# A branch hint for the final jump, eight separate PSUM banks for the tail's products, and three accumulations handed to ScalarE and GpSimd

## The chip, the core and the metric

The kernel runs on one core of a Trainium2 chip. The core has TensorE (PE in the profile, its weight loads PEld) for matrix products into PSUM, VectorE (DVE) and ScalarE (ACT), which read PSUM and SBUF, GpSimd (POOL), used here on SBUF alone, and SyncE (SP), which issues nearly all DMAs. Each engine has its own queue of instructions and runs it in order; engines wait for each other through semaphores. A jump is an instruction of every engine's queue. The metric is the device time of one launch in microseconds (us), the median over runs.

## What is computed

The input is one sequence of 2048 rows with 512 columns. Two branches read the same x, and a gate mixes them row by row:

```python
g = _sigmoid((x * gate_w).sum(-1, keepdims=True))
a = _A_ref(x, A_wq, A_wk, A_wv, A_wo)   # attention: 32 heads of 16, one k and one v for all heads
b = _B_ref(x, B_w1, B_w2)               # silu(x @ w1) @ w2, 1792 hidden columns
return g * a + (1 - g) * b
```

Attention is softmax(q k / 4) v for each head and then a product with wo (512x512). All inputs and the output are float32.

## The kernel before

Products are made from pairs of float16 parts: every operand is split into a leading part and a rest, and three matmuls (leading by leading, leading by rest, rest by leading) stand for one.

**Two passes.** `first_pass` splits with fixed powers of two as scales. While it runs it collects extreme values, checks them against limits, and writes one integer, `flag`. `second_pass` is the same computation with scales worked out from the data. All engines load `flag` (L1632) and jump (L1633) over the code of `second_pass` if it is 0. It is 0 with these inputs, so a run consists of the first pass, the jump and the end of the program. The second pass is thousands of instructions long, so the jump's target lies far behind the jump.

**The main loop.** The sequence is cut into four chunks `c` of 512 rows, the heads into four groups `o` of eight, each handled in two rounds: 32 rounds (`rounds`) of 16 steps. In a step TensorE makes scores into a tile S (`scores`, L1381), ScalarE exponentiates them (L1387), and TensorE multiplies the result with v into two banks pv (`sums`, L1485). VectorE makes the rests of the exponentials (`low`, L1406). The feed-forward products and the projections with wo fill TensorE's spare slots (`f_slot`, L1027). PSUM has eight banks of 512 float32 per partition: two S tiles of two banks each, the banks pv0 and pv1, and two banks pm.

**Order.** The queues' order is made by a planner in Python that keeps an estimated clock for each engine (`pe[0]`, `dve[0]`, `act[0]`, `pool[0]`). Work for VectorE is entered by `put(duration, ready, due, function)`; `choice` picks the task with the earliest due time. The planner's clocks decide the order alone; on the chip, semaphores decide the times.

**The end of a round.** `norm_a` normalizes a round: `out_of_psum` transposes pv0 and pv1 into T and U (L1303, L1304), `joined` adds and scales (L1309 to L1311), `quotient` divides (L1325 to L1327), and after the second round of a head group `turned` transposes back and splits the result O in two (L1333 to L1336). In the last round (`late`) VectorE does all of it; before, GpSimd does L1309 to L1311, L1335 and L1336. O feeds `out_proj`.

**Outputs.** For each block of 128 output rows there is a tile `acc` in SBUF, to which six products of the last chunk are added in turn: four feed-forward parts (`ffn_o`, gate `g1`), a projection of the first three head groups, and one of the last group (`out_proj`, gate `gg`). `evict_out` enters the addition as a task of VectorE, `add_out` (L1001), which reads the product from PSUM, multiplies it by the gate and adds it to `acc`; after the last part it issues the output's DMA on SyncE's queue (L1004). `parts[n]` counts what a block has, `n_parts(n)` what it needs.

**The tail.** When all scores are issued, a first loop finishes the sums that are left, a second the feed-forward product that is under way, and a third makes the eight last products, each with full 128x128 matmuls (L1031): the last feed-forward part of four row blocks, six matmuls each, and the projections of the last head group, three each. Before each product all of VectorE's open tasks are entered. The generator `spaces` names the PSUM bank that each product goes to: the first banks of two S tiles, their second banks, then two banks pm, then S again. A tile is one unit for the waits, so a product in the second bank of an S tile waits for the readers of its first bank.

Of the kernel before, what the change touches and what calls it, by code (L numbers as in the profile page):

```python
# [6 lines left out]
F32 = mybir.dt.float32  # L7
# [5 lines left out]
AF = mybir.ActivationFunctionType  # L13
OP = mybir.AluOpType
# [159 lines left out]
def kernel(  # L174
# [21 lines left out]
    nc = tc.nc  # L196
    _, S, D = x.shape
# [19 lines left out]
    g1 = consts.tile([128, NKT], F32)  # L217
# [693 lines left out]
    def attention(ctx, scale_of, t_scale, shifts, split_pieces, chores, q_todo, bounds, early, gates_, later):  # L911

        wp = ctx.enter_context(tc.tile_pool(name="wp", bufs=1, reuse_waits="tile"))
        pS = ctx.enter_context(tc.tile_pool(name="pS", bufs=2, space=PSUM, reuse_waits="tile"))
        pO = ctx.enter_context(tc.tile_pool(name="pO", bufs=1, space=PSUM, reuse_waits="tile"))
# [4 lines left out]
        pe, act, dve, pool, turn = [0.0], [0.0], [0.0], [0.0], [0.0]  # L920
# [11 lines left out]
        def put(dur, ready, due, f, hard=False, low=None, turns=False):  # L932

            tasks.append([due, ready, dur, f, hard, low, turns])
            return tasks[-1]

        def pool_until(t):

            while pooled and max(pool[0], pooled[0][0]) <= t:
                ready, dur, f = pooled.pop(0)  # L940
                pool[0] = turn[0] = max(pool[0], ready, turn[0]) + dur
                pool[0] += 0.08
                if f:
                    f(pool[0])

        def on_pool(durs, f=None):
            for n, dur in enumerate(durs):
                pooled.append((dve[0] + 0.1, dur, f if n == len(durs) - 1 else None))

        def do(t):  # L950
            tasks.remove(t)
            dve[0] = max(dve[0], t[1])
            pool_until(dve[0])
            if t[6]:
                dve[0] = turn[0] = max(dve[0], turn[0]) + t[2]
            else:
                dve[0] += t[2]
            t[3]()
# [30 lines left out]
        accs, parts, given = {}, {}, {}  # L989
        n_parts = lambda n: len(GF) + 1 + (n // 4 == NCH - 1)  # L990

        def add_out(c, t, po, gate):
            n = c * 4 + t
            if n not in accs:
                assert n < ACCS or parts[n - ACCS] == n_parts(n - ACCS)
                accs[n] = wp.tile([128, D], F32, name="acc", bufs=ACCS)
            a = accs[n]
            if n not in parts:
                nc.vector.tensor_scalar(a, po, gate[:, n:n + 1], None, op0=OP.mult)
            else:  # L1000
                nc.vector.scalar_tensor_tensor(a, po, gate[:, n:n + 1], a, op0=OP.mult, op1=OP.add)  # L1001
            parts[n] = parts.get(n, 0) + 1
            if parts[n] == n_parts(n):
                nc.sync.dma_start(out[n * 128:n * 128 + 128], a)  # L1004

        def evict_out(c, t, gate):

            def evict(po):
                return put(0.75, pe[0] + 0.2, pe[0] + 0.9, lambda: add_out(c, t, po, gate), True)

            return evict
# [53 lines left out]
        def out_proj(c, O, t):  # L1065
            need(wo, 0)
            given[c] = given.get(c, 0) + 1
            return Out([(lambda i, b, m, n=32, o=o: O[o][b, i, t * 128 + m:t * 128 + m + n],
                         lambda j, b, o=o: wo_s[b, j, o]) for o in O],
                       evict_out(c, t, gg))  # L1070
# [215 lines left out]
        def norm_a(i, pv, rb, key):  # L1286

            while (t := next((v for v in tasks if v[3] is of_v[0]), None)):
                do(t)
            T, U = wp.tile([128, 512], F32, name="T"), wp.tile([128, 512], F32, name="U")  # L1290
            z = U.rearrange("p (a b) -> p a b", b=32)
            if rb == 0:
                state["C"] = wp.tile([128, 16, 32], F32, name="C")
            C = state["C"][:, :, 16 * rb:16 * rb + 16]

            late = i == len(rounds) - 1
            eng = nc.vector if late else nc.gpsimd

            def out_of_psum():
                while of_norm[0] in tasks:  # L1300
                    pool_until(1e8)
                    do(of_norm[0])
                nc.vector.transpose(T, pv[0])  # L1303
                nc.vector.transpose(U, pv[1])  # L1304
                closed[i] = dve[0] + 0.06
                joined()

            def joined():
                eng.tensor_tensor(U, T, U, op=OP.add)  # L1309
                eng.tensor_tensor(C[:, :, 1:16], z[:, :, 1:16], z[:, :, 17:32], op=OP.add)  # L1310
                eng.tensor_tensor(z[:, :, 1:1 + DIGITS], z[:, :, 17:17 + DIGITS], mu[:, :, 1:].to_broadcast([128, 16, DIGITS]), op=OP.mult)  # L1311
                if late:
                    dve[0] += 1.2
                q = of_norm[0] = put(0.80, dve[0], dve[0], quotient, turns=not late)
                if not late:
                    q[0], q[1] = 1e9, 1e9

                    def summed(t):
                        q[0], q[1] = t + 4, t

                    on_pool((1.28, 0.7, 0.41), summed)

            def quotient():
                r = wp.tile([128, 16, 1], F32, name="rr")
                nc.vector.reciprocal(r, z[:, :, 16:17])  # L1325
                nc.vector.tensor_reduce(C[:, :, 0:1], z[:, :, 0:1 + DIGITS], axis=AX.X, op=OP.add)
                nc.vector.tensor_tensor(C, C, r.to_broadcast([128, 16, 16]), op=OP.mult)  # L1327
                if rb:
                    of_norm[0] = put(0.7, dve[0], dve[0] + 4 * (not late), turned)

            def turned():
                OT = wp.tile([128, 512], F32, name="T")
                nc.vector.transpose(OT, state["C"].rearrange("p a b -> p (a b)"))  # L1333
                O = wp.tile([128, 2, 512], F16, name="O", bufs=NO)
                eng.tensor_copy(O[:, 0], OT)  # L1335
                eng.tensor_tensor(O[:, 1], OT, O[:, 0], op=OP.subtract)  # L1336
                Os[key] = O
                c, o = key
                if late:
                    dve[0] += 1.12  # L1340

                if o == NO - 1 or c == NCH - 1 and o == NO - 2:
                    all_ = {q: Os.pop((c, q)) for q in range(NO) if (c, q) in Os}
                    ready = lambda end: urgent.extend((c, end, lambda t=t: out_proj(c, all_, t)) for t in range(4))
                else:
                    ready = None
                if not late:
                    on_pool((0.61, 1.16), ready)
                elif ready:
                    ready(dve[0])  # L1350

            closed[i] = None
            closing[:] = [put(1.4, pe[0] + 0.25, pe[0] + 0.6, out_of_psum, True)]
# [9 lines left out]
        probs, ends, low_end, lows, of_v, of_norm = {}, {}, {}, {}, [None], [None]  # L1363
# [173 lines left out]
        while p < n_s:  # L1537
# [22 lines left out]
            n = sums_next(room, False)  # L1560
            near = left_in_round() <= way.near
            fresh = T_.going and T_.n - T_.i >= way.fresh
            if n is not None and near and not fresh and last_unit(n) and behind < way.lastb:
                n = None
            if n is None and behind >= way.hurry:
                n = sums_next(room)
# [16 lines left out]
                    p += 1  # L1583


        while first[0] < len(steps):
            serve(pe[0])
            n = sums_next(9.0)
            if n is not None:
                sums(n)  # L1590
            elif f_ready():
                f_slot()
            else:
                pe[0] += 0.05
# [8 lines left out]
        def spaces():  # L1603
            while True:
                pair = [pS.tile([128, 2, 512], F32, name="S") for _ in range(2)]
                for f in range(2):
                    for sc in pair:
                        yield sc[:, f]
                yield pM.tile([128, 512], F32, name="pm")
                yield pM.tile([128, 512], F32, name="pm")  # L1610

        space = spaces()
        while not ended[0] or tasks:
            pool_until(1e8)
            while tasks:
                do(min(tasks, key=lambda t: t[0]))
            o = ahead.pop() if ahead else next(seq, 0)
            if o == 0:
                ended[0] = True
            elif o is None:  # L1620
                pe[0] += 0.05
            else:
                if not hasattr(o, "bank"):
                    o.bank = next(space)
                for n in range(o.n):
                    o.whole(n, n == 0, n == o.n - 1)
                    pe[0] += SLOT
                o.evict(o.bank)
# [1 line left out]
    with tc.manual_schedule():  # L1630
        first_pass()
    over = nc.values_load(flag[0:1, 0:1], min_val=0, max_val=1)  # L1632
    with tc.If(over > 0):  # L1633
        second_pass()


# [25 lines left out]
```

## Time and profile before

| what | value |
|---|---|
| median of three runs | 1031.53 us |
| lowest and highest run | 1030.94 and 1031.7 us |
| profiled execution, time | 1032.32 us |
| its span, first to last instruction | 1030.4 us |
| granted TensorE clock | 0.999 |

The profile shows one execution. Its span leaves out what lies ahead of the first and behind the last instruction, here 1.9 us. A row of the order of time gives start and duration in us, engine, line, operation, output and input tiles, shapes, a count, and in brackets the idle time ahead of it with what ended it. The chain of waits goes back from the last instruction, at each step to what released it or to the instruction ahead of it on its engine. A q behind an engine's name (SPq) marks what its sequencer does: jumps, semaphore waits, DMA issues. Queues q8 and q14 carry instruction fetches, q1 the data.

### The profile page before, as it was taken

The page shows a single profiled execution, that of the slowest core. Times are in us where ns is not written, and L with a number is a line of the kernel's source. Part 1 is how long each engine was busy: PE and PEld are TensorE (multiplying, and loading weights), DVE is VectorE, ACT ScalarE, POOL GpSimd, SP SyncE. Part 2 cuts the span into 40 slices and gives each one's busy share as a digit, 9 for nine tenths or more (in the row PEclk, how much of TensorE's full clock was granted, in tenths as well). Part 3 has the DMA queues.
Part 4 walks back from the last instruction along what each step waited for, and adds up shares of the span by engine and source line. Part 5 has one row for each costly group of instructions (what it writes and reads, how often), then busy time and mean ns, then how long its engine had stood idle before and what let it go on. Part 6 is the DMA issues. An engine that isn't in the chain of part 4 may idle for free.

```text
span 1030.4 us, 65694 instructions
## 1 busy us (share of the span) xinstructions
PE 1012.3 (98%) x31006; PEld 575.8 (56%) x31006; DVE 862.4 (84%) x802; ACT 993.2 (96%) x1116; POOL 396.2 (38%) x281
## 2 busy tenths in 40 slices
PE   7999999999999999999999999999999999999996
PEld 5455555555555565565555555556555565555553
DVE  6698988989989888889877887777988887788886
ACT  5899999999999999999999999999999999999992
POOL 2024326222131351627444145353426236281920
PEclk9999999999999999999999999999999999999999
DMA  7211211100000100000000010000000010000001
GB/s 258 90 58 58 68 40 63 53 12 23 12 15 32 33 22 13 12 19 7 22 12 33 23 42 6 21 12 13 28 12 7 18 43 12 13 12 12 5 5 45
DMA packets 23905, 33.08 MB, mean 32 GB/s; under 512 B 5113, under 2 KB 13594, under 8 KB 23626
## 3 DMA queue, kind: packets, MB, share of 16 engines
q1 hardware_dynamic: 23098, 28.63, 8.5%
q8 instruction: 244, 4.00, 1.5%
q14 instruction: 35, 0.29, 0.1%
q10 hardware_dynamic: 432, 0.07, 0.0%
q0 software_dynamic: 96, 0.10, 0.0%
HBM read 20.25 MB, written 8.52 MB: 28 GB/s over the span
## 4 chain that ended last, share of the span: by engine, by line
PE 62%; ACT 23%; DVE 8%; issue 4%; DMA 1%; POOL 0%; SPq 0%; ACTq 0%; DVEq 0%
PE pm L1027 22%; ACT P L1387 22%; PE pv L1485 21%; PE S L1381 15%; DVE L L1406 4%; ACT e L1041 1%; PE pt L462 1%; PE pm L1031 1%; DMA xn<-in_A_x_dram 1%; PE pk L562 1%; DVE e L1046 0%; PE S L1031 0%; DVE acc L1001 0%; DMA raw<-in_B_w_dram 0%; DVE U L1304 0%
## 5 line engine op out<-in xcount | busy, mean ns | idle before, releaser
L1387 ACT ACTIVATE P<-S 128x1024 f32<-128x1024 f32 x1024 | 956.6, 1093 | 3.5 <-PE S L1381 1.7
L1406 DVE TENSOR_TENSOR L<-P 128x2048 f16<-128x2048 f32 x232 | 555.9, 2407 | 45.5 <-ACT P L1387 45.0
L1381 PE MATMUL S<-qb,KT 50*32 50x512 f16 x8192 | 435.9, 380 | 2.4 <-DVE KT L582 0.5
L1381 PEld LDWEIGHTS <-KT 50*32 50x32 f16 x8192 | 194.9, 89 | 240.3 <-issue 154.3
L1485 PE MATMUL pv<-P,VF 64*32 64x512 f32 (+1 forms) x5744 | 317.7, 498 | 0.0
L1027 PE MATMUL pm<-w2s,H 64*32 64x512 f16 x5184 | 261.3, 375 | 0.2 <-issue 0.2
L1027 PE MATMUL pm<-xs,w1s 64*32 64x512 f16 x5376 | 250.9, 375 | 0.7 <-DVE e L1046 0.4
L1309 POOL TENSOR_TENSOR U<-T,U 128x512 f32<-128x512 f32 x31 | 81.2, 2618 | 302.8 <-DVE U L1304 302.8
L1048 POOL CAST H<-e 128x512 f16<-128x512 f32 x56 | 66.0, 1178 | 215.5 <-DVE e L1046 177.7
L1027 PEld LDWEIGHTS <-H 64*32 64x32 f16 x5184 | 115.3, 92 | 41.9 <-issue 3.2
L1027 PEld LDWEIGHTS <-w1s 64*32 64x32 f16 x5376 | 109.6, 92 | 50.6 <-issue 8.1
L1485 PEld LDWEIGHTS pv<-P,VF 64*32 64x32 f32 x5744 | 114.2, 106 | 35.5 <-issue 5.7
L1049 POOL TENSOR_TENSOR H<-e,H 128x512 f16<-128x512 f32 x56 | 113.6, 2029 | 4.5
L1485 PE MATMUL pv<-P,VP 64*32 64x512 bf16 x1832 | 100.9, 387 | 0.2 <-DVE U L1304 0.2
L1485 PE MATMUL pv<-L,VP 64*32 64x512 f16 x1832 | 97.2, 374 | 0.6 <-DVE L L1406 0.4
L1027 PE MATMUL pm<-xs,wqs 64*32 64x512 f16 x1152 | 84.7, 375 | 0.0
L1485 PEld LDWEIGHTS <-VP 64*32 64x32 f16 x3664 | 63.2, 92 | 30.9 <-issue 9.9
L1046 DVE SCALAR_TENSOR_TENSOR e<-e,pm 128x512 f32<-128x512 f32 x56 | 38.4, 685 | 36.9 <-ACT e L1041 36.7
L1027 PE MATMUL pm<-wo_s,O 64*32 64x512 f16 x1440 | 66.3, 375 | 0.0
L1001 DVE SCALAR_TENSOR_TENSOR acc<-pm,g,acc 128x512 f32<-128x512 f32 x44 | 32.9, 747 | 17.5 <-PE pm L1027 17.2
L1310 POOL TENSOR_TENSOR C<-U 128x240 f32<-128x240 f32 x31 | 43.3, 1398 | 2.4
L1311 POOL TENSOR_TENSOR U<-U,mu 128x96 f32<-128x96 f32 x31 | 42.8, 1382 | 2.4
(173 smaller groups left out, 523.6 us busy)
## 6 DMA issues: line engine op xcount, KB each, us to landing
qb<-qd SPq DMA_DIRECT2D x189, 32.0 KB
raw<-in_B_w_dram SPq DMA_DIRECT2D x22, 256.0 KB
xn<-in_A_x_dram SPq DMA_DIRECT2D x8, 512.0 KB
out_dram<-acc SPq DMA_DIRECT2D x16, 256.0 KB
qd<-qx SPq DMA_DIRECT2D x12, 256.0 KB
w1r<-in_B_w_dram SPq DMA_DIRECT2D x2, 512.0 KB
raw<-in_A_wo_dram SPq DMA_DIRECT2D x4, 256.0 KB
qb<-sh SPq DMA_DIRECT2D x62, 2.0 KB
```

Of the source, the lines that this page charges most:

```text
L1001: nc.vector.scalar_tensor_tensor(a, po, gate[:, n:n + 1], a, op0=OP.mult, op1=OP.add)
L1027: nc.tensor.matmul(self.bank[32 * m:32 * m + 32], l(i, rows, 32 * m), r(j, rows), start=first, stop=last)
L1046: nc.vector.scalar_tensor_tensor(e, e, 1.0, ph, op0=OP.add, op1=OP.mult)
L1048: nc.gpsimd.tensor_copy(H[:, 0], e)
L1049: nc.gpsimd.tensor_tensor(H[:, 1], e, H[:, 0], op=OP.subtract)
L1309: eng.tensor_tensor(U, T, U, op=OP.add)
L1310: eng.tensor_tensor(C[:, :, 1:16], z[:, :, 1:16], z[:, :, 17:32], op=OP.add)
L1311: eng.tensor_tensor(z[:, :, 1:1 + DIGITS], z[:, :, 17:17 + DIGITS], mu[:, :, 1:].to_broadcast([128, 16, DIGITS]), op=OP.mult)
L1381: nc.tensor.matmul(sc[32 * m:32 * m + 32, f], KT[b:b + 50, k0:k0 + 32], qtile[i][b:b + 50, j], start=True, stop=True)
L1387: nc.scalar.activation(P[:, 2 * j:2 * j + 2], sc, AF.Exp, scale=scale_of(c, o))
L1406: nc.vector.tensor_tensor(L[s], P, upper(P), op=OP.subtract)
L1485: nc.tensor.matmul(pvs[i][h][32 * j:32 * j + 32, cols], a[r], b[r, j, cols], start=start, stop=rest == n)
```

## The change

1. A branch hint. Where all scores have been issued and the first of the three last loops begins, each of the five engines gets a hint that the jump labelled "over" is likely taken. The conditional gets that label and is laid out so that the second pass follows the jump and the end of the program is the jump's target.
2. `spaces` gives out all eight banks before any is used again: the first banks of two S tiles, pm, pv0, pv1, pm, and then the second banks of the two S tiles.
3. In the third loop (`ending`), a feed-forward product that is not the last part of its row block goes through `add_by_pool`: ScalarE multiplies it by the gate into a tile `e` in SBUF, and GpSimd adds `e` to `acc`. Projections, and whatever comes last for its block, stay with VectorE.
4. In the last round `quotient` and, after it, `turned` get a due time ahead of everything else.

```diff
+        ending = [False]
+
+        def add_by_pool(c, t, po, gate):
+            n = c * 4 + t
+            e = wp.tile([128, D], F32, name="e", bufs=2)
+            nc.scalar.activation(e, po, AF.Identity, scale=gate[:, n:n + 1])
+            nc.gpsimd.tensor_tensor(accs[n], accs[n], e, op=OP.add)
+            parts[n] += 1
+
         def evict_out(c, t, gate):
 
             def evict(po):
+                if ending[0] and gate is g1 and parts[c * 4 + t] < n_parts(c * 4 + t) - 1:
+                    return add_by_pool(c, t, po, gate)
                 return put(0.75, pe[0] + 0.2, pe[0] + 0.9, lambda: add_out(c, t, po, gate), True)
...
-                q = of_norm[0] = put(0.80, dve[0], dve[0], quotient, turns=not late)
+                q = of_norm[0] = put(0.80, dve[0], dve[0] if not late else -9.0, quotient, turns=not late)
...
-                    of_norm[0] = put(0.7, dve[0], dve[0] + 4 * (not late), turned)
+                    of_norm[0] = put(0.7, dve[0], dve[0] + 4 if not late else -9.0, turned)
...
+        if early:
+            tc.mark_branch_hint_location("over", "LikelyTaken", engines=[e.engine for e in (nc.sync, nc.tensor, nc.vector, nc.scalar, nc.gpsimd)])
         while first[0] < len(steps):
...
                 pair = [pS.tile([128, 2, 512], F32, name="S") for _ in range(2)]
-                for f in range(2):
-                    for sc in pair:
-                        yield sc[:, f]
+                for sc in pair:
+                    yield sc[:, 0]
                 yield pM.tile([128, 512], F32, name="pm")
+                for h in range(2):
+                    yield pO.tile([128, 512], F32, name=f"pv{h}")
                 yield pM.tile([128, 512], F32, name="pm")
+                for sc in pair:
+                    yield sc[:, 1]
 
         space = spaces()
+        ending[0] = True
...
-    with tc.If(over > 0):
+    with tc.If(over > 0, label="over", preferred_fallthrough_block=True):
         second_pass()
```

## The prediction

> **What bounds the kernel now.** I read the page first. TensorE is busy for nearly all of the span, and nothing in the change touches the loop that fills it, so what matters is where TensorE is idle: the last stage.
>
> ```profile
> span 1030.4 us, 65694 instructions
> PE 1012.3 (98%) x31006; PEld 575.8 (56%) x31006; DVE 862.4 (84%) x802; ACT 993.2 (96%) x1116; POOL 396.2 (38%) x281
> ```
>
> The second view is the chain of waits that ended last, cut to its final stage (start, length, what).
>
> ```profile
> 1011.73 0.71 DVE T L1303
> 1012.44 0.61 DVE U L1304
> ...
> 1015.27 0.66 DVE acc L1001
> ...
> 1017.04 0.69 DVE O L1336
> 1017.74 0.67 DVE acc L1001
> 1018.41 0.04 issue
> 1018.45 2.10 PE S L1031 x9
> 1020.55 1.29 PE pm L1031 x6
> 1021.85 1.96 PE S L1031 x9
> ...
> 1023.83 0.75 DVE acc L1001
> ```
>
> From 1011.73 the chain runs on VectorE, not TensorE: the last attention sums go through one VectorE sequence, and two accumulations (L1001, 0.66 and 0.67 us) sit in it, one ahead of the steps that make O and one behind O (L1336). The second releases TensorE. The third view, the order of time, shows what TensorE waited for (start, duration, engine, line, tiles, count, idle before).
>
> ```profile
> 1014.53 2.76 PE L1031 MATMUL S<-w2s,H 128*128 128x512 f16 x12
> ...
> 1018.45 1.46 PE L1031 MATMUL S<-w2s,H 128*128 128x512 f16 x6 [1.16 <-DVE acc L1001]
> ...
> 1019.74 0.81 PE L1031 MATMUL S<-wo_s,O 128*128 128x512 f16 x3
> ...
> 1023.83 0.75 DVE L1001 SCALAR_TENSOR_TENSOR acc<-S,g,acc 128x512 f32<-128x512 f32 x1 [0.50 <-PE S L1031]
> ```
>
> I call the eight last products F0 to F3 (feed-forward, six matmuls each) and P0 to P3 (projection of the last head group, three each). These rows and the chain read: F0 and F1 in one run, F2 after 1.16 us of idling, then P0 (in S), P1 and P2 (pm, six matmuls in the chain), P3 and F3 (S, nine). F2 goes into the second bank of F0's S tile and waits until VectorE has read F0, which VectorE does only after O.
>
> The last view is what follows the final accumulation: the last output transfer, the instructions of the jump and the waits behind it (L1633) with shortest/median/longest ns and first and last start, and the DMA queues in two half microseconds (1027.0 to 1027.5, 1027.5 to 1028.0).
>
> ```profile
> 1024.61 0.63 SPq L1004 DMA_DIRECT2D out_dram<-acc  x1
> ```
>
> ```profile
> L1633 SPq EVENT_SEMAPHORE  x8: 17/17/17, 1028.2 to 1028.7; - x8
> ...
> L1633 ACTq COMPARE_BRANCH  x1: 50/50/50, 1009.4 to 1009.4; - x1
> ...
> L1633 DVEq COMPARE_BRANCH  x1: 72/72/72, 1024.5 to 1024.5; - x1
> L1633 SPq COMPARE_BRANCH  x1: 45/45/45, 1025.3 to 1025.3; - x1
> ...
> L1633 DVEq EVENT_SEMAPHORE  x1: 21/21/21, 1027.4 to 1027.4; - x1
> ```
>
> ```profile
> q8 instruction: 1, 0.02, 11.6%
> q1 hardware_dynamic: 3, 0.00, 2.2%
> ```
>
> ```profile
> q14 instruction: 1, 0.01, 4.0%
> ```
>
> SyncE jumps at 1025.3 and runs its next instruction at 1028.2. In those 2.9 us it waits for no data; the one packet moved between 1027.5 and 1028.0 is an instruction fetch (q14). VectorE loses the same 2.9 us behind its jump (1024.5 to 1027.4). The last three packets of the output (q1) move between 1027.0 and 1027.5. So SyncE starts to check that the output has landed about a microsecond after it did, and then needs from 1028.2 to the end at 1030.4, 2.2 us, for its waits and the closing handshake.
>
> **The change part by part.**
>
> *Eight banks (spaces).* F0, F1, F2, P0 to P3 and F3 get S, S, pm, pv, pv, pm, S, S. F2's bank is now a pm whose accumulation was long past; P0 and P1 use the pv banks, whose last readers L1303 and L1304 end at 1013.05, and which are needed from 1018.4. Twelve matmuls from 1014.53 at 0.215 us each (1018.45 to 1019.74 holds six) let F2 start at 1017.11 in place of 1018.45: **1.34 us** earlier, if O is ready in time.
>
> *The due times of the two late steps.* Quotient and turn now come ahead of any other work of VectorE in the planner's order. The accumulation at 1015.27 moves behind O, so O is complete at 1017.74 - 0.66 = 1017.1. P0 needs it at 1017.11 + 1.29 = 1018.4; it is hidden by F2. The order of products stays: the planner lets the projections in once its TensorE clock has passed the end of the turn, and one accumulation less (0.75 us by its own reckoning) ahead of the turn leaves that end still behind F1 and ahead of F2. The moved accumulation reads the other pm bank, is done by 1017.9, and P2 wants that bank at 1019.7.
>
> *F0 to F2 by ScalarE and GpSimd.* Three accumulations leave VectorE. What is added is three activations from PSUM and three GpSimd additions of 128x512 f32. Their rows:
>
> ```profile
> L584 ACT ACTIVATE KT<-pt,m_one x2: 680/684/687, 26.5 to 27.1; 128x512 f16<-128x512 f32 x2
> ```
>
> ```profile
> L1309 POOL TENSOR_TENSOR U<-T,U x31: 1273/3237/3448, 71.1 to 986.9; 128x512 f32<-128x512 f32 x31
> ```
>
> ScalarE is free (it has reached its jump at 1009.4), takes 0.68 us each, and needs no new table, since the same function ran at 26.5 among the others. GpSimd's addition has two prices, 1.27 and 3.24 us. The order of time shows what decides:
>
> ```profile
> 438.24 1.29 POOL L1309 TENSOR_TENSOR U<-T,U 128x512 f32<-128x512 f32 x1 [3.45 <-DVE U L1304]
> ```
>
> ```profile
> 438.77 0.69 DVE L1122 SCALAR_TENSOR_TENSOR qx<-pm,qx 128x512 f16<-128x512 f32 x1
> ```
>
> ```profile
> 986.90 3.24 POOL L1309 TENSOR_TENSOR U<-T,U 128x512 f32<-128x512 f32 x1 [7.70 <-DVE U L1304]
> ```
>
> ```profile
> 986.74 2.25 DVE L1406 TENSOR_TENSOR L<-P 128x2048 f16<-128x2048 f32 x1
> ```
>
> Beside a VectorE instruction with one input in PSUM and one in SBUF (L1122) the addition takes 1.29; beside L1406, whose inputs are both in SBUF, it ends only when that one has ended and about a full addition later. The accumulations of the tail have L1122's form, and VectorE's rows from 1011.73 on hold no L1406. So I take 1.28, with 3.24 as the other end. One instruction of L1406's kind is left, the subtraction L1336 until 1017.1. The Trainium skill, "SBUF — State Buffer", section "Who interferes with whom", says that GpSimd and a VectorE instruction with two SBUF inputs take turns on one port pair, whole instruction by whole instruction; these four rows agree, and by it only the first addition loses about 0.4 us.
>
> The schedule: F0 is complete at 1016.0 (six steps of 0.215 and the 0.18 by which twelve overrun in 2.76), scaled by 1016.7, added 1017.2 to 1018.5; F1 by 1019.9; F2 by 1021.2 (0.08 between additions). VectorE's accumulations stand in a fixed order P0, P1, P2, P3, F3, so each waits behind P2's, which waits for F2's addition: P2 starts at 1021.3, the next ones 0.67 apart as at 1017.74: F3 at 1022.6. By TensorE alone F3's product ends 1.34 earlier and its accumulation could start at 1022.5. The final accumulation thus moves from 1023.83 to 1022.6: **1.2 us**, bounds 1.34 (TensorE decides) and a loss (rival 3). SyncE's last transfer follows it at the same 0.03 us.
>
> *The hint.* Without the fetch, SyncE goes through its first waits and stands at the one for the last transfer. I price issue to landing: now 1024.61 to the last packets at 1027.0 to 1027.5, 2.4 to 2.9, with a TensorE fetch of 16 KB (q8) among them. I take 2.6. Then come the waits behind it, of the 2.2 us without some 0.4 for those already done: 1.8. So 4.4 from issue to end against 1030.4 - 1024.6 = 5.8: **1.4 us**; with 2.9 and all 2.2 it is 0.7, with 2.2 and 1.8 it is 1.8. Cost: one more instruction on each engine's queue, at the end of the scores. Nearest rows are the jumps themselves, 45 to 72 ns; TensorE is on the path there, so 0.05 us is lost (bounds 0 and 0.07). Queued behind it are the last three steps' sums. The fetch that it triggers is a packet or so per engine, while no output moves.
>
> Sum: 1.2 + 1.4 - 0.05 = 2.55 us. The profiled execution took 1032.32, 1.9 more than its span and 0.8 above the median; the span becomes 1027.9, that execution's time 1029.8, and the median 1031.53 - 2.55 = **1029.0**.
>
> **The rivals.**
>
> 1. *The hint does nothing for SyncE.* For it: the hint stands behind the last load of q in SyncE's queue, long before its jump, and no row shows a fetched block kept that long. Against: SyncE has a handful of instructions between. Then only the tail gains: 1031.53 - 1.2 = 1030.3. The Trainium skill, "Runtime: NRT & Kernel Launch", section "Instruction fetch mechanics", says that prefetch is purely sequential in a window of two pages and that a taken branch outside it forces a fetch. The 2.9 us rows agree with the second half; taken strictly, the first half gives this rival.
>
> 2. *The tail gains nothing.* GpSimd's additions take about 1.7 us each, F2's ends at 1022.4, and F3's accumulation starts where it does today. For it: the spread of L1309; against: no L1406 in the tail. Time 1031.53 - 1.35 = 1030.2.
>
> 3. *Slower: GpSimd becomes the bound.* Place: P2's accumulation, waiting for the third addition. At 3.24 us each from 1017.2 that addition ends at 1027.1, F3's accumulation starts at 1028.5, 4.7 later than now; with the hint's 1.4 the time is 1034.8. It decides from about 2.2 us per addition on. For it: the median of L1309 is 3.24; against: the slow row stood beside L1406, which the tail lacks.
>
> 4. *A fetch stall inside the tail*, if the hinted block displaces the one that the engine runs into next: 2.9 us on VectorE or TensorE, 1031.53 - 2.55 + 2.9 = 1031.9. For it: the stall's size at the jump; against: no stall like it in the tail's rows now.
>
> **How the numbers follow.** Forecast 0.67, rivals 0.14, 0.08, 0.08, 0.03. The forecast's own range is 1028.4 (1.34 and 1.8) to 1029.7 (1.2 and 0.7). A measurement of this kernel tells about 0.2%, 2.1 us, from no change, so faster means below 1029.47: nine tenths of the forecast, 0.60. Same is the rest of it with rivals 1, 2 and 4, 0.32; slower is rival 3, 0.08. The range starts 0.2 lower for the spread of the runs and goes to 1030.4, with which it takes in rivals 1 and 2.
>
> **What would show it.** In the changed profile F2 should start near 1017.1 without idle before it; GpSimd should show three additions near 1.3 us, the first up to 0.4 longer; P2's accumulation should start near 1021.3, the last near 1022.6; SyncE's first instruction behind its jump should follow within 0.2 us, and its eight waits should be split by one gap; the span should end about 4.4 us after the last transfer's issue. Additions over 2 us, a gap of 2.9 us still behind SyncE's jump, or a new idle stretch of TensorE between 1009 and 1017 would prove it wrong.

## The result and the profile after

| | before | after |
|---|---|---|
| time, median of 13 runs each | 1031.53 us (1030.84 to 1032.21) | 1029.02 us (1028.01 to 1029.96) |
| ratio | | 0.9978, 95% interval 0.9971 to 0.9986 |
| profiled execution: its time | 1032.32 us | 1028.67 us |
| its span | 1030.4 us | 1026.8 us |

The kernel became 2.5 us faster, 0.2%. The first view of the kernel after is the head of its page.

```profile
span 1026.8 us, 65712 instructions
...
PE 1011.9 (99%) x31006; PEld 579.2 (56%) x31006; DVE 861.0 (84%) x799; ACT 995.7 (97%) x1119; POOL 394.9 (38%) x284
```

TensorE does the same 31006 matmuls in the same 1012 us. VectorE has three instructions fewer, ScalarE and GpSimd three more each: the three accumulations that moved. The gain has to lie in what stands around the matmuls, so the next view is the order of time of the last stage (start, duration, engine, line, operation, tiles, count, idle before). VectorE's first step in it, the first transposition of the last round, started at 1011.00.

```profile
1011.00 0.72 DVE L1314 STREAM_TRANSPOSE T<-pv 128x512 f32<-128x512 f32 x1
...
1013.81 2.76 PE L1042 MATMUL S<-w2s,H 128*128 128x512 f16 x12
...
1015.37 0.69 ACT L1011 ACTIVATE e<-S,g 128x512 f32<-128x512 f32 x1 [6.00 <-PE S L1042]
1015.78 0.69 DVE L1347 TENSOR_TENSOR O<-T,O 128x512 f16<-128x512 f32 x1
1016.14 3.93 POOL L1012 TENSOR_TENSOR acc<-acc,e 128x512 f32<-128x512 f32 x3 [23.54 <-ACT e L1011]
1016.39 0.75 DVE L1001 SCALAR_TENSOR_TENSOR acc<-pm,g,acc 128x512 f32<-128x512 f32 x1
1016.41 1.46 PE L1042 MATMUL pm<-w2s,H 128*128 128x512 f16 x6
1017.70 1.46 PE L1042 MATMUL pv<-wo_s,O 128*128 128x512 f16 x6
...
1020.10 0.75 DVE L1001 SCALAR_TENSOR_TENSOR acc<-pm,gg,acc 128x512 f32<-128x512 f32 x1
1020.29 1.46 PE L1042 MATMUL S<-w2s,H 128*128 128x512 f16 x6
...
1021.85 0.75 DVE L1001 SCALAR_TENSOR_TENSOR acc<-S,g,acc 128x512 f32<-128x512 f32 x1 [0.34 <-PEq L1650]
```

F2 (pm, 1016.41) now follows F0 and F1 (S, 1013.81) without idling; before there were 1.16 us between them. O is complete at 1016.47, while F2 runs, and P0 (pv, 1017.70) starts as F2 ends. F3's product runs from 1020.29 to 1021.75, and its accumulation starts right behind it, after VectorE has idled for 0.34 us: TensorE decides when the last accumulation starts. (The bracket names what TensorE's sequencer, PEq, did at that time.) The three GpSimd additions take 3.93 us together and end at 1020.07, and P2's accumulation starts 0.03 us later. So GpSimd has only some 0.3 us to spare, VectorE's idle time ahead of the last accumulation.

The next view is the line of the jump in the kernel after, with the rows of SyncE and VectorE (count: shortest/median/longest ns, first and last start).

```profile
L1650 SPq EVENT_SEMAPHORE  x8: 17/17/17, 1023.5 to 1025.1; - x8
...
L1650 DVEq COMPARE_BRANCH  x1: 90/90/90, 1022.8 to 1022.8; - x1
L1650 SPq COMPARE_BRANCH  x1: 70/70/70, 1023.0 to 1023.0; - x1
...
L1650 DVEq EVENT_SEMAPHORE  x1: 21/21/21, 1023.5 to 1023.5; - x1
```

SyncE jumps at 1023.0 and is at its first wait at 1023.5; before, that took 2.9 us. Its eight waits now spread over 1.6 us (before 0.5): they really wait for the output. From the last of them to the end of the span it is 1.7 us, in both kernels.

To compare runs I use one number, **the meter**: from the start of the last round's first transposition on VectorE (T<-pv; L1303 before, L1314 after) to the end of the span. Before it is 1030.4 - 1011.7 = 18.7 us, after 1026.8 - 1011.0 = 15.8 us. So the stage that the change touches became 2.9 us shorter. The profiled spans differ by 3.7 because the part ahead of the meter also was 0.7 us shorter in this execution; that part differs by more than that from run to run (below).

### The profile page after: what moved, and what is told of

Same layout as the page of the kernel before. It is cut to its first block, busy times and chain, and to the rows that moved or that the text cites. A ratio compares the mean times of both kernels' runs of the same rounds, so it can differ in the third digit from the quotient of the medians.

```text
span 1026.8 us, 65712 instructions
## 1 busy us (share of the span) xinstructions
PE 1011.9 (99%) x31006; PEld 579.2 (56%) x31006; DVE 861.0 (84%) x799; ACT 995.7 (97%) x1119; POOL 394.9 (38%) x284
## 5 line engine op out<-in xcount | busy, mean ns | idle before, releaser
L1320 POOL TENSOR_TENSOR U<-T,U 128x512 f32<-128x512 f32 x31 | 79.0, 2549 | 307.9 <-DVE U L1315 307.9
L1038 PEld LDWEIGHTS <-w1s 64*32 64x32 f16 x5376 | 112.4, 92 | 49.5 <-issue 8.0
L1001 DVE SCALAR_TENSOR_TENSOR acc<-pm,g,acc 128x512 f32<-128x512 f32 x44 | 32.9, 747 | 17.6 <-PE pm L1038 17.3
L1038 PEld LDWEIGHTS <-wqs 64*32 64x32 f16 x1152 | 36.2, 92 | 11.2 <-issue 1.1
```

The costliest lines, as they stand in the source:

```text
L1038: nc.tensor.matmul(self.bank[32 * m:32 * m + 32], l(i, rows, 32 * m), r(j, rows), start=first, stop=last)
```

## The experiments

The theory was that two independent gains add, one from the tail (issue of the last transfer 1.2 us earlier) and one from the hint (issue to end 1.4 us shorter). Its rivals: that only one of them is real, that a due time or the move to GpSimd does the tail's work instead of the banks, and that the hint on SyncE alone would do. The meters of all runs, in us, with the start of the last accumulation counted from the same point, and the time's ratio to the kernel before where more than one run was timed. The number in brackets is the kernel before, timed beside it:

| run | last accumulation | meter | median us (before) | ratio, 95% interval |
|---|---|---|---|---|
| before | 12.1 | 18.7 | 1031.53 | |
| after | 10.85 | 15.8 | 1029.02 (1031.53) | 0.9978 [0.9971, 0.9986] |
| after_again | 10.84 | 15.8 | 1028.61 (1031.25) | 0.9974 [0.9965, 0.9983] |
| e1_hint_only | 12.1 | 17.7 | 1032.23 (1031.26) | 1.0005 [0.9993, 1.0018] |
| e1b_hint_only_again | 12.1 | 17.5 | 1030.69 (1031.25) | 0.9992 [0.9983, 1.0001] |
| e2_tail_only | 10.84 | 17.2 | 1030.33 (1031.26) | 0.9992 [0.9983, 1.0002] |
| e4_hint_sync_only | 10.84 | 16.4 | one run, 1027.94 | |
| e4b_hint_sync_only_again | 10.84 | 17.2 | 1029.42 (1031.25) | 0.9979 [0.9970, 0.9988] |
| e5_hint_not_sync | 10.84 | 17.3 | one run, 1032.26 | |
| e6_banks_only | 10.79 | 15.9 | one run, 1029.32 | |
| e7_no_due | 10.89 | 15.9 | one run, 1028.75 | |
| e8_pool_twice | 12.86 | 17.9 | one run, 1033.14 | |
| e9_old_banks | 10.79 | 16.4 | one run, 1028.74 | |
| e10_last_in_halves | 11.04 | 16.3 | 1029.44 (1031.25) | 0.9983 [0.9974, 0.9992] |

### The hint alone

```diff
 (kernel before)
+        if early:
+            tc.mark_branch_hint_location("over", "LikelyTaken", engines=[e.engine for e in (nc.sync, nc.tensor, nc.vector, nc.scalar, nc.gpsimd)])
...
-    with tc.If(over > 0):
+    with tc.If(over > 0, label="over", preferred_fallthrough_block=True):
```

> The kernel before with the hint and the label of the jump alone; the tail's products, banks and additions stay as before. Meter for all runs: the stretch from the start of the last round's first transposition on VectorE (T from pv) to the end of the span; it was 18.7 us before (1011.72 to 1030.4) and 15.8 after (1011.00 to 1026.8), and from the issue of the last output transfer to the end it was 5.8 and 4.15 us. Theory (two separate gains, hint and tail): the last accumulation starts 12.1 us into the meter as before, issue to end is 4.1 to 4.4 us, the meter 17.0 to 17.3 us, the time about 1.5 us under before. Rival 1 (the hint does nothing, the tail carries all): meter 18.7, time as before.

SyncE's rows at the jump in this run:

```profile
L1635 SPq EVENT_SEMAPHORE  x8: 17/17/17, 1027.3 to 1029.4; - x8
...
L1635 SPq COMPARE_BRANCH  x1: 70/70/70, 1026.7 to 1026.7; - x1
```

The 2.9 us behind the jump are gone (1026.7 to 1027.3), and the meter is 1.0 us shorter. That is less than expected (17.7 in place of 17.0 to 17.3): SyncE no longer stalls, but the output lands as late as before, 2.5 us after its issue (2.6 before). The section on the engines comes back to this. The time wasn't shorter at all: 1.0005, with an interval that holds no change. The place where it went is ahead of the meter. The view of the exponentials' line gives the length of the main loop, from the first to the last start; here are the kernel before and this run.

```profile
L1387 ACT ACTIVATE P<-S x1024: 1013/1086/1267, 33.4 to 1009.0; 128x1024 f32<-128x1024 f32 x171
```

```profile
L1387 ACT ACTIVATE P<-S x1024: 1015/1084/1274, 31.2 to 1010.7; 128x1024 f32<-128x1024 f32 x171
```

The loop took 975.6 us before and 979.5 us here. Either it is longer because of the hint, or it varies by itself. The same kernel was run again to tell.

> The kernel before with the hint alone, once more: its first run had the shorter end (meter 17.7 against 18.7) and still no gain in time, since its main loop, first to last exponential, took 979.5 us against 975.6 in the profile of before. Theory A (the loop's length differs from execution to execution by a few us whatever the hint, most of it between 185 and 210 us where weights are loaded): the meter is 17.2 to 17.7 again, the median about 1.0 to 1.5 us under before. Theory B (hints on the computing engines delay instruction fetches in the main loop): the loop is 979 us or more again and the median is 0.5 to 1 us over before.

```profile
L1387 ACT ACTIVATE P<-S x1024: 1016/1086/1273, 31.2 to 1008.4; 128x1024 f32<-128x1024 f32 x171
```

The loop now took 977.2 us and the median was 1030.69, 1.5 us less than the same kernel's the first time, with a meter of 17.5. So the loop's length varies with the hint unchanged, and a median on another occasion can be off by more than a microsecond. Beside the kernel before it is 0.6 us less, where 1.0 to 1.5 were expected, and the interval still touches 1: in time alone, the hint's part is not established by itself. In the meter it is 1.0 and 1.2 us.

### The tail alone

```diff
 (kernel after)
-        if early:
-            tc.mark_branch_hint_location("over", "LikelyTaken", engines=[e.engine for e in (nc.sync, nc.tensor, nc.vector, nc.scalar, nc.gpsimd)])
...
-    with tc.If(over > 0, label="over", preferred_fallthrough_block=True):
+    with tc.If(over > 0):
```

> The changed kernel without the hint, its label and the layout request. Theory: the last accumulation starts 10.85 us into the meter as in the changed kernel, SyncE loses 2.9 us behind its jump, issue to end is 5.6 to 5.8 us, the meter 17.2 to 17.5 us, the time about 1.25 us under before. Rival 2 (the tail gains nothing): the last accumulation starts at 12.1, meter 18.7.

This run's first transposition, last accumulation and last transfer, and its jump on SyncE:

```profile
1010.59 0.72 DVE L1314 STREAM_TRANSPOSE T<-pv 128x512 f32<-128x512 f32 x1
...
1021.43 0.75 DVE L1001 SCALAR_TENSOR_TENSOR acc<-S,g,acc 128x512 f32<-128x512 f32 x1 [0.34 <-PEq L1648]
```

```profile
1022.21 0.33 SPq L1004 DMA_DIRECT2D out_dram<-acc  x1
```

```profile
L1648 SPq EVENT_SEMAPHORE  x8: 17/17/17, 1025.5 to 1026.1; - x8
...
L1648 SPq COMPARE_BRANCH  x1: 45/45/45, 1022.6 to 1022.6; - x1
```

The last accumulation starts 10.84 us into the meter, 1.27 earlier than before, and the 2.9 us behind the jump are back. The last transfer's issue takes 0.33 us, where it took 0.63 before; SyncE jumps 0.3 us earlier for it. That part can't be put down to the tail: the issue takes 0.33 us in e1 too, with the tail of before, and 0.64 in e9 (below). What sets it is not shown. The meter is 1.55 us shorter than before. With the hint's 1.0 to 1.2 that makes 2.6 to 2.7; together they give 2.9 in the changed kernel and in its repeat:

> The changed kernel, on the chip of the other runs of this call. Theory A: median about 2.5 us under before, meter 15.8, loop 975.5 to 978. Theory B: the loop is longer than with the hint on SyncE alone by 2 us or more, so that this kernel is no faster than that one.

It gave a meter of 15.8 again and the time 0.9974 [0.9965, 0.9983]. In the meter the two gains add to within 0.2 to 0.4 us, and no single one accounts for the whole. In time, each alone has an interval that touches 1 (0.9992 [0.9983, 1.0002] for the tail); only both together are clear of the noise.

### Which part of the tail counts

Three kernels undo parts of the tail; all carry the hint. e6 keeps the banks alone, e7 takes back the due times, e9 the banks. Each of the three was profiled once.

```diff
 (e6: kernel after, banks and hint only)
-                if ending[0] and gate is g1 and parts[c * 4 + t] < n_parts(c * 4 + t) - 1:
-                    return add_by_pool(c, t, po, gate)
...
-                q = of_norm[0] = put(0.80, dve[0], dve[0] if not late else -9.0, quotient, turns=not late)
+                q = of_norm[0] = put(0.80, dve[0], dve[0], quotient, turns=not late)
...
-                    of_norm[0] = put(0.7, dve[0], dve[0] + 4 if not late else -9.0, turned)
+                    of_norm[0] = put(0.7, dve[0], dve[0] + 4 * (not late), turned)
```

> The changed kernel without the ScalarE and GpSimd additions and without the two early due times: of the tail's changes only the eight banks are left (and the hint). All of VectorE's nine accumulations are back, with the one ahead of O. From the durations of the trace VectorE, freed from waiting, would reach F3 at 10.6 us in the meter (O at 6.0, then eight steps of 0.66 us), and TensorE brings F3 at 10.8. Theory C (the banks alone carry the tail's gain): the last accumulation starts at 10.8 to 10.9, meter 15.8. Theory D (the work taken from VectorE is needed too): it starts at 11.4 or later.

```diff
 (e7: kernel after, with the last two of these edits only)
```

> The changed kernel with the old due times: one accumulation of 0.66 us stands ahead of O again, so O is complete at about 6.1 us in the meter in place of 5.5, and TensorE wants it at 6.7. Theory C (O is hidden by F2): the last accumulation starts at 10.85, nothing lost. Rival (the first GpSimd addition starts at 5.1, ahead of the subtraction that completes O, and keeps it out until 6.4): O at 7.1, the first projection 0.4 us late, the last accumulation at 11.2 to 11.3.

```diff
 (e9: kernel after, with the banks of before)
-                for sc in pair:
-                    yield sc[:, 0]
+                for f in range(2):
+                    for sc in pair:
+                        yield sc[:, f]
                 yield pM.tile([128, 512], F32, name="pm")
-                for h in range(2):
-                    yield pO.tile([128, 512], F32, name=f"pv{h}")
                 yield pM.tile([128, 512], F32, name="pm")
-                for sc in pair:
-                    yield sc[:, 1]
```

> The changed kernel with the old order of banks: F2 shares F0's tile again, P0 shares F1's, F3 shares P0's. F0 is now read by ScalarE, which is done at 5.06 us in the meter, and TensorE reaches F2 at 5.41. Theory C': either of the two edits alone removes the wait, so F2 starts without a gap and the last accumulation at 10.85, meter 15.8. Theory D': the shared tile still costs a wait, with a gap ahead of F2 or P0 and the last accumulation at 11.2 or later.

The order of time of e6, with its first transposition, its products F0 to F2 and the accumulations of VectorE that count:

```profile
1011.56 0.72 DVE L1312 STREAM_TRANSPOSE T<-pv 128x512 f32<-128x512 f32 x1
...
1014.37 2.76 PE L1040 MATMUL S<-w2s,H 128*128 128x512 f16 x12
...
1016.97 1.46 PE L1040 MATMUL pm<-w2s,H 128*128 128x512 f16 x6
...
1017.49 1.40 DVE L1001 SCALAR_TENSOR_TENSOR acc<-S,g,acc 128x512 f32<-128x512 f32 x2
...
1022.35 0.75 DVE L1001 SCALAR_TENSOR_TENSOR acc<-S,g,acc 128x512 f32<-128x512 f32 x1 [0.17 <-PE S L1040]
```

F2 starts without a gap although VectorE reads F0 and F1 only at 1017.49, because F2's bank no longer is theirs. VectorE then does all accumulations itself and still is ready for the last one when TensorE is: it starts at 10.79 us, as early as with GpSimd, and the meter is 15.9. **The banks alone bring the tail's whole gain** in the meter. In e9 the banks are the old ones, and F0 is read by ScalarE:

```profile
1010.51 0.72 DVE L1314 STREAM_TRANSPOSE T<-pv 128x512 f32<-128x512 f32 x1
...
1013.32 4.06 PE L1042 MATMUL S<-w2s,H 128*128 128x512 f16 x18
...
1021.30 0.75 DVE L1001 SCALAR_TENSOR_TENSOR acc<-S,g,acc 128x512 f32<-128x512 f32 x1 [0.29 <-PE S L1042]
```

All 18 matmuls of F0 to F2 run without a gap here too, since ScalarE releases F0's tile early; the last accumulation again starts at 10.79. Each of the two edits, the banks or the move to ScalarE and GpSimd (e9 keeps the due times), removes the idle time without the other, so together they bring no more than one. What e9 loses (16.4 in place of the expected 15.8) lies behind the last accumulation: its last issue takes 0.64 us, and a 16 KB fetch moves among its output, as the view from 1020.8 to 1022.4 shows (packets, MB, share of the DMA engines).

```profile
q8 instruction: 1, 0.02, 6.1%
```

In e7 the due times of before let an accumulation back in ahead of O. The order of time there:

```profile
1011.06 0.72 DVE L1314 STREAM_TRANSPOSE T<-pv 128x512 f32<-128x512 f32 x1
...
1016.19 2.95 POOL L1012 TENSOR_TENSOR acc<-acc,e 128x512 f32<-128x512 f32 x2 [23.93 <-ACT e L1011]
1016.38 1.64 DVE L1347 TENSOR_TENSOR O<-T,O 128x512 f16<-128x512 f32 x1
...
1017.76 0.59 PE L1042 MATMUL pv<-wo_s,O 128*128 128x512 f16 x2
```

The subtraction L1347, with both inputs in SBUF, stands for 1.64 us instead of 0.69 when GpSimd's first addition started ahead of it: the addition delays VectorE here, where in the kernel after VectorE was first. So O is complete only near 7.0 us, about as late as the rival had it (7.1). P0 nevertheless starts 6.70 us into the meter, just as in the kernel after (1017.70 - 1011.00); at its recorded start the recorded end of L1347 (1018.02) is still to come, so its first matmuls seem not to need all of O. The last accumulation is 0.04 us later, since P2's now waits 0.32 us for GpSimd's third addition, which uses up VectorE's idle time. The due times are worth nothing measurable in this kernel; they keep GpSimd's chain from becoming the limit.

### GpSimd's work made longer

```diff
 (kernel after)
             nc.scalar.activation(e, po, AF.Identity, scale=gate[:, n:n + 1])
             nc.gpsimd.tensor_tensor(accs[n], accs[n], e, op=OP.add)
+            nc.gpsimd.tensor_tensor(e, e, e, op=OP.add)
```

The sum that is added here is used by nothing.

> The changed kernel with a second addition of the same size (e to itself, its result is used by nothing) behind each of GpSimd's three, so that one row block costs it 2.55 us in place of 1.27. If P2's accumulation waits for the third real addition, that one ends near 11.9 us in the meter in place of 9.06, P2 follows at 11.95, F3 at 13.3, and the meter is 18.2 us: the whole tail gain and more is lost. If the accumulations do not wait for GpSimd, the last one stays at 10.85.

The order of time of this run, from the third product's addition on (its first transposition started at 1013.45):

```profile
1023.47 1.26 POOL L1012 TENSOR_TENSOR acc<-acc,e 128x512 f32<-128x512 f32 x1
1024.76 0.75 DVE L1001 SCALAR_TENSOR_TENSOR acc<-pm,gg,acc 128x512 f32<-128x512 f32 x1 [1.58 <-POOL acc L1012]
...
1026.31 0.75 DVE L1001 SCALAR_TENSOR_TENSOR acc<-S,g,acc 128x512 f32<-128x512 f32 x1
```

VectorE idles 1.58 us ahead of P2's accumulation, and the releaser is GpSimd's third addition (1023.47 + 1.26 = 1024.73). The last accumulation starts at 12.86 (expected 13.3: the extra addition takes 1.04 us, not as long as the real one), 2.0 us later than in the kernel after, and the meter grows by 2.1. This is the place and the mechanism of the prediction's slower rival, at a price that the change didn't pay.

### On which engines the hint counts

```diff
 (kernel after; e4 and e4b: SyncE alone)
-            tc.mark_branch_hint_location("over", "LikelyTaken", engines=[e.engine for e in (nc.sync, nc.tensor, nc.vector, nc.scalar, nc.gpsimd)])
+            tc.mark_branch_hint_location("over", "LikelyTaken", engines=[e.engine for e in (nc.sync,)])
 (e5: all but SyncE)
+            tc.mark_branch_hint_location("over", "LikelyTaken", engines=[e.engine for e in (nc.tensor, nc.vector, nc.scalar, nc.gpsimd)])
```

> The changed kernel with the hint on SyncE alone. Theory (only SyncE's fetch is on the path): SyncE's first wait runs 0.5 us behind its jump; VectorE pays 2.9 us behind its own jump and arrives at 14.75 us in the meter, just where SyncE comes to wait for it, so the meter is 15.8 to 15.9 us, up to 16.5 if the other engines' fetches delay packets of the output. Rival (all engines' fetches count): meter 17 or more.

> The changed kernel with the hint on the four other engines and not on SyncE. Theory: SyncE's first wait runs 2.9 us behind its jump, near 14.9 us in the meter, after the output has landed, and the meter is 17.0 to 17.2 us: the hint's whole gain is lost. Rival: the gain comes from any of the others, meter near 15.8 us.

> The changed kernel with the hint on SyncE alone, timed. Its first look gave meter 16.4, 0.6 more than with all hints, because the last output landed 0.6 us later among the other engines' fetches. Theory A: median 0.6 us over the changed kernel's in this call. Theory B: median 1 us or more under it.

The jump in e5:

```profile
L1650 SPq EVENT_SEMAPHORE  x8: 17/17/17, 1028.2 to 1028.8; - x8
...
L1650 SPq COMPARE_BRANCH  x1: 45/45/45, 1025.1 to 1025.1; - x1
```

and in e4:

```profile
L1650 SPq EVENT_SEMAPHORE  x8: 17/17/17, 1022.2 to 1024.3; - x8
...
L1650 DVEq COMPARE_BRANCH  x1: 72/72/72, 1021.5 to 1021.5; - x1
L1650 SPq COMPARE_BRANCH  x1: 70/70/70, 1021.7 to 1021.7; - x1
L1650 DVEq EVENT_SEMAPHORE  x1: 21/21/21, 1025.0 to 1025.0; - x1
```

Without its hint SyncE waits 3.1 us behind the jump, and the meter is 17.3, about that of the tail alone. VectorE's unhinted jump in e4 likewise takes 3.5 us (1021.5 to 1025.0). Both kernels have the conditional's new layout, so the layout without the hint does not remove the stall. With SyncE's hint alone that wait is 0.5 us, but the meter missed the expected 15.8 to 15.9: 16.4, and 17.2 when the same kernel ran again. The median of that second run, 1029.42, is 0.8 us above the changed kernel's beside it (1028.61; 0.6 was expected). SyncE's last wait starts later: 14.6 us into e4's meter (1024.3, with the first transposition at 1009.68) and 15.5 into e4b's, against 14.1 in the kernel after. The output itself lands later. The DMA view of the 2.5 us from the issue of the last transfer shows which instruction fetches move beside it (packets, MB, share of the 16 engines), first in e4 from 1021.3 on, then in the kernel after from 1022.6 on.

```profile
q8 instruction: 1, 0.02, 2.8%
q14 instruction: 3, 0.02, 2.7%
```

```profile
q14 instruction: 2, 0.02, 2.2%
```

In e4 (and in e4b) four instruction fetches move beside the last output, one of them TensorE's 16 KB; in the kernel after only two small ones do, as in e5, where TensorE had its hint. The kernel before had a 16 KB fetch and two small ones there.

Is it the number of fetches or TensorE's? The traces of all 14 runs tell something. From the issue of the last transfer to its last packet it is 1.7 to 1.9 us in the six runs in which TensorE's 16 KB fetch starts at least 2.5 us ahead of that issue (after, after_again, e5, e6, e7, e8). It is 2.1 to 3.3 us in the eight in which one starts between 1.7 us ahead of the issue and 0.9 us behind it (before, e1, e1b, e2, e4, e4b, e9, e10). Four of these eight, e1, e1b, e9 and e10, have all five hints, and only two small fetches beside the last transfer, like the kernel after. So the late landing goes with TensorE's fetch, and the hint on TensorE doesn't always keep one away: where TensorE's remaining fetch falls differs from kernel to kernel. SyncE's hint removes the stall in every run that has it; that the output also lands early in the kernel after holds for this kernel's arrangement. That the fetch causes the later landing is inferred from these times; no run moved it alone. In e4b the 16 KB fetch starts 0.5 us later in the meter than in e4, and the output lands 0.8 us later; the rest stays open.

### The last product in halves

```diff
 (kernel after; F3 alone, in place of its product, accumulation and transfer)
+            for h in range(2):
+                cols = slice(256 * h, 256 * h + 256)
+                bank = o.bank if h == 0 else pM.tile([128, 512], F32, name="pm")
...
+                nc.vector.scalar_tensor_tensor(e[:, 0:256], bank[:, 0:256], g1[:, n:n + 1], accs[n][:, cols], op0=OP.mult, op1=OP.add)
+                nc.sync.dma_start(out[n * 128:n * 128 + 128, cols], e[:, 0:256])
```

> The changed kernel with the very last product F3 made in two halves of 256 columns in two banks, each half added by VectorE into a tile of its own and sent out by itself. The end waits for the last addition and the last transfer, so both halve: the last addition starts about 0.1 us later (more weight loads) and takes 0.41 in place of 0.75 us, the last transfer moves half the bytes. Theory: last issue 0.25 us earlier in the meter (11.4), landing 0.2 us quicker, meter 15.3, time 0.4 us under the changed kernel. Rival (transfer time is latency, and the extra issue on SyncE eats the gain): meter 15.7 or more.

The order of time of this run, second half's accumulation and the issues of both halves:

```profile
1021.06 0.47 DVE L1637 SCALAR_TENSOR_TENSOR e<-pm,g,acc 128x256 f32<-128x256 f32 x1
...
1021.17 1.12 SPq L1638 DMA_DIRECT2D out_dram<-e  x2
```

A miss. The second half's accumulation is short (0.47 us in place of 0.75) but the two issues take 1.12 us on SyncE, so the last transfer is issued 0.26 us later than in the kernel after, and half the bytes didn't land sooner: 2.1 us from issue to last packet. The meter is 0.5 us longer. What halving costs by itself stays open, since TensorE's 16 KB fetch starts 1.7 us ahead of the last issue here, among the output, as it doesn't in the kernel after. No version beat the kernel after in the meter or in a median of several runs.

## Why the prediction was right

The time came out at 1029.02, as forecast (1029.0), and both gains have about the size given to them, by the mechanisms given. That the two times agree to 0.02 us is luck: two medians of one kernel differed by 1.5 us (e1 and e1b), and some terms below miss in opposite directions. Step by step:

- **F2 without idling, O under its cover.** Right. Counted from the first transposition, F2 starts at 5.41 us (before 6.72): 1.31 us earlier, where the prediction had 1.34. O is complete at 5.47 (predicted 5.4) and P0 starts at 6.70 (predicted 6.7).
- **GpSimd's additions.** Right in size, 1.27 each; the first took 1.47, so it lost 0.2 us rather than 0.4. Its recorded start (1016.14) lies inside L1347 (1015.78 to 1016.47). The row of L1347 in e7, 1.64 us, agrees with the section of the Trainium skill, "SBUF — State Buffer", that the prediction named ("Who interferes with whom"): here GpSimd was first, and VectorE's subtraction ended only 0.55 us behind the addition's 1.27 us.
- **Which engine decides.** The prediction let GpSimd decide by 0.1 us, with F3's accumulation at 1022.6 against 1022.5 by TensorE. TensorE decides; GpSimd's third addition ends at 9.07 us of the meter and not at 9.5, since its chain began 0.3 us earlier. The last accumulation moved by 1.26 us (12.11 to 10.85) against the 1.2 given.
- **What brings the tail's gain.** The prediction credited the banks with F2's early start and gave the due times and GpSimd parts of their own. The runs show that the banks suffice (e6), that the due times are worth nothing beside the other edits (e7), and that the move to ScalarE and GpSimd does the same work a second time (e9). It adds a chain with some 0.3 us of slack (e7, e8).
- **The hint's gain.** The size is right, its terms are not. Issue to end went from 5.82 us (1030.43 - 1024.61) to 4.15 (1026.77 - 1022.62): 1.7 against the 1.4 predicted. 0.3 of it is the shorter last issue, which is there without the hint as well (e2), so beside the new tail the hint's own part is near 1.4; with the tail of before it is 1.0 to 1.2 (e1, e1b). The prediction made its 4.4 of 2.6 from the issue to the last packet and 1.8 behind it. In the kernel after, the last packet moves 1.7 us after the issue, with no 16 KB fetch in its way. SyncE's waits go on only 0.6 us after that packet, a term that the prediction left out, and then 1.8 us follow to the end. The two misses, 0.9 too much and 0.6 too little, nearly cancel.
- **Where the hint runs, and its cost.** Wrong. The description of the change and the prediction put it at the end of the scores, and the prediction charged 0.05 us on TensorE's path. The line of the program's ends in the kernel after shows the hints at 0.7 to 0.8 us, 4 us ahead of TensorE's first matmul, where they cost the tail nothing:

```profile
L1675 SPq BRANCH_PREFETCH_HINT  x1: 60/60/60, 0.7 to 0.7; - x1
...
L1675 PEldq BRANCH_PREFETCH_HINT  x1: 50/50/50, 0.8 to 0.8; - x1
```

- **Behind the jump.** SyncE's next instruction was to follow within 0.2 us; it took 0.5. That cost nothing, as SyncE then waits for the output anyway.
- **The rivals.** The first, that the hint does nothing for SyncE, fell with e1 and e5. The rule that stood beside it, sequential prefetch alone (the Trainium skill, "Runtime: NRT & Kernel Launch", "Instruction fetch mechanics"), does not hold for a hinted jump; the rule's second half, that a taken branch outside the window forces a fetch, agrees with the 2.6 to 3.5 us behind each unhinted one. The second, that the tail gains nothing, fell with e2. The third is real as a mechanism (e8) but the additions stayed at 1.3 to 1.5 us. The fourth, a fetch stall in the tail, shows nowhere: between 1015 and 1023 no group of matmuls has idle time ahead of it, and VectorE idles there only ahead of products that are still being made.
- **The sum.** 2.55 us predicted, 2.9 in the meter, 2.5 and 2.6 in the medians. The difference of 0.3 to 0.4 between meter and medians isn't explained; it is smaller than the main loop's variation.

## What to carry to other kernels

Where the end of a kernel is a jump over code that hasn't run, look at what the engines do between the jump and their next instruction, and hint the jump on all engines, and then look where the fetches that are left fall: here one of 16 KB among the last output went with a landing 0.4 to 1.5 us later, and four of those eight runs had all hints set. When two edits of a tail remove the same idle time, try each alone: here giving every product its own PSUM bank did all of it in the meter, and the move to ScalarE and GpSimd only added a chain to watch. For gains near a microsecond in a kernel of a millisecond, measure the stage itself and repeat the run, since one median can be off by as much as the gain.

## What the runs showed that was not expected

- A hint executed at 0.7 to 0.8 us still worked at the jump at 1018 to 1023 us, after all the code in between had been fetched. With all five hints the page's count of instruction packets falls by one on TensorE's queue and by four on the others'; here are the kernel before and the kernel after.

```profile
q8 instruction: 244, 4.00, 1.5%
q14 instruction: 35, 0.29, 0.1%
```

```profile
q8 instruction: 243, 3.98, 1.7%
q14 instruction: 31, 0.25, 0.1%
```

  With SyncE's hint alone it was 244 and 34, with all but SyncE's 243 and 32: one packet less for each hinted engine. So the last fetch ahead seems to go to the jump's target, in place of one for the code behind the jump and another at the jump. That is read from the counts alone.
- A hinted jump isn't free. To the next instruction it was 0.5 us on SyncE and ScalarE, 0.6 on VectorE and 0.8 on GpSimd in the kernel after (in the other runs up to 0.7 on ScalarE and 1.8 on GpSimd); without the hint it was 2.9 us before and 2.6 to 3.5 in the other runs.
- The length of the main loop, whose code none of these edits touch, lay between 975.6 and 979.5 us in the profiled executions. What sets it was not tried. Nor was the conditional's new layout with no hint at all.
